# A two-layer attention kernel on one core: its written-out schedule replaced by another (order of the queues, engines, buffers, GpSimd's waits, TensorE's fillers)

## The chip, the cores and the metric

One core of one Trainium2 chip runs the whole kernel. The metric is the time of one execution on the device in microseconds, the median of several runs. The engines are named as in the profile: PE (TensorE's matmuls), PEld (its weight loads), DVE (VectorE), ACT (ScalarE), POOL (GpSimd), SP (SyncE, which only issues DMAs here).

## The reference

x has 2048 tokens of 512 numbers in bf16. Two layers follow each other, and each layer is an A block and a B block with a residual sum around each:

```python
x = x + _A_ref(_layernorm(x), A_wq, A_wk, A_wv, A_wo, A_beta)
x = x + _B_ref(_layernorm(x), B_wqkv, B_w_phi, B_wo)
```

and then the same two lines again. A has 32 heads of 16 numbers and 4 segments of 512 tokens. Within a segment it is causal softmax attention; beside it stands a memory (M, z) that the segments before have summed up, and a gate per head mixes the two:

```python
logits = einsum('bhqd,bhkd->bhqk', qs, ks) * scale + mask
a_dot  = softmax(logits) @ vs
a_mem  = (phi(qs) @ M) / (phi(qs) @ z + 1e-06)
o = g * a_mem + (1 - g) * a_dot
M = M + phi(ks).T @ vs;  z = z + sum(phi(ks))
```

with phi(t) = t + 1 where t > 0 and exp(t) elsewhere. B is linear attention over all tokens: queries and keys go through a 16x16 matrix per head, then softmax(t) and softmax(-t) side by side; kv and z are sums over all tokens, and o = (phi_q @ kv) / (phi_q @ z + 1e-06). Both blocks end in a product with a 512x512 matrix.

## The kernel before, in words

All of x lies in SBUF (`X`, 16 tiles of 128 tokens). The program is written as a list of 3416 small operations, numbered in the order in which the Python code adds them; an operation is one instruction of DVE, ACT, POOL or a DMA, or a few matmuls. In each layer the code goes through four segments: LayerNorm (`ln`: statistics, rstd by POOL's pow, xn on DVE, then a transpose by DMA or by PE), Q, K and V (`a_proj`), score products, Exp and masks and the product with V (`a_att`), the memory (`a_state`, `a_mem`), the output product and the residual sum (`a_out`); then for B the keys (`b_keys`), queries (`b_queries`) and, when all tokens are summed, the output (`b_out`). The output of B of the first layer is spread over the second layer's segments.

What an engine does next is not decided by the order of the Python code. Four tables are written out in the file, and `replay` reads them:

- `ORDER` lists the numbers of all operations. Each engine's queue (PE, ACT, DVE, POOL, SP) is the operations on it in this order, and each queue runs strictly in order. A number with 10000 added is interleaved, two matmuls at a time, with the PE operation before it. A negative number is a filler: matmuls on the zero tile `warm` (line 1431), whose result nobody reads; -401 stands for 25 of them.
- `ENGINE` has a letter for each of the 568 operations that could run on more than one engine (a, d, p, s for ACT, DVE, POOL, SP).
- `SLOTS` has the number of the buffer, or the PSUM bank, for each tile in the order of use. An operation waits until all users of the buffer's tile before are done.
- `AFTER` has pairs (x, y): operation x waits for y as well. In all pairs x is on POOL and y on DVE.

`finalize` makes semaphores of all this. The lines that the times below are told by:

```python
k, p = int(next(slots), 36), t.pool
...
self.queues[op.on].append(op.i)
...
for x, y in AFTER:
    ops[x].need.add(y)
```

Operations that the prediction speaks of, by number: 0, 1, 4, 5 load the first four tiles of x (X0 and X2 by ACT's queue, X1 and X3 by SP's, 128 KB each); 2 and 3 load the halves of `WA_k` (256 KB, ACT and SP), 6 and 7 those of `WA_q`, 8 and 9 those of `WA_v`; 10 loads beta (8 KB, ACT). SP alone loads 11 (X4 to X7, 512 KB), 12 (`wphi`, 16 KB), 13 and 14 (the raw B weights, 512 KB each), 15 (`WA_o`), 16 (`WB_v`), 17 and 18 (X8 to X11, X12 to X15) and 19 (`WB_o`). 20 sets `warm` to zero, 81 and 82 clear the two `ktok` buffers (line 767), all on DVE. 84 is the first K product, which reads both halves of `WA_k`. In `a_att`, the mask of the odd keys (line 1110) is one of those that may run on DVE or POOL; the mask of the even ones (line 1113) is always POOL's. Line 520 is the helper that issues every matmul, 579 the copy out of PSUM, 585 the DMA transposes, 601 PE's transposes, 1104 the Exp of the scores.

## Time and profile before

| | |
|---|---|
| time, median of 3 runs | 479.87 us (479.76 to 480.22) |
| span of the profiled execution | 479.8 us, which stands for its own time: 0.07 us under the median |
| busy: PE, DVE, ACT, POOL | 464.4, 428.1, 430.7, 261.0 us |
| weight loads (PEld) | 320.1 us |
| DMA | 35.86 MB, of which 6.32 MB read from HBM and 2.10 MB written |
| most instructions of one kind | L1104 Exp, 288 x 1068 ns, 282.4 us busy |
| masks of the odd keys, L1110 | 127 on POOL (697 ns each), 129 on DVE (364 ns each) |
| DMA transposes, L585 | 100, issue to landing 3.0 to 5.6 us, median 3.3 |

The page has one execution: busy time per engine, the span in 40 slices, DMA queues, the chain of work that ended last (followed back from the last instruction, at each step to what released it), the costliest groups of instructions by line, and the DMA issues. A group's row ends in its busy time, the mean length of one, and the engine's idle time ahead of it with what ended it. Consecutive instructions of an engine overlap a little, so busy time over count is less than the mean length. The end of a matmul is modelled, so PE's busy time holds some waiting too.

### The profile page before, as it was taken

Reading aid. Unit: us, or ns where it says so; the run is one execution under the profiler, and the core shown is the slowest. Engines: PE = TensorE matmul, PEld = TensorE weight load, DVE = VectorE, ACT = ScalarE, POOL = GpSimd, SP = SyncE. Lnnn points to the kernel's source line nnn. Section 1 sums busy time; section 2 is a strip of 40 time slices with the busy share of each in tenths; the row PEclk is TensorE's granted clock in tenths of the full one; section 3 lists DMA queues with packets and bytes.
Section 4 is the critical chain, followed back from the end, with each engine's and each line's share of the span. In section 5 each row is a group of like instructions: output and inputs, shape, how many; then the busy total and the mean of one; then the engine's idle time right before and its main releaser. Section 6 shows DMA issues by size and latency. Waiting matters only on the chain.

```text
span 479.8 us, 19249 instructions
## 1 busy us (share of the span) xinstructions
PE 464.4 (97%) x8324; PEld 320.1 (67%) x8324; DVE 428.1 (89%) x1021; ACT 430.7 (90%) x668; POOL 261.0 (54%) x420
## 2 busy tenths in 40 slices
PE   8999989999999999999999999999999999999997
PEld 7776667667856567557687666766865657665763
DVE  6999999989998988599999899999998879978785
ACT  3999999999999999986799899899999999999743
POOL 3577657646756576410246485784776578761100
PEclk9999999999999999999999999999999999999999
DMA  8978752225411232232257407236145112402376
GB/s 264 160 196 132 127 78 46 46 48 78 59 23 25 46 68 47 19 39 47 55 88 93 62 9 124 58 53 81 39 56 89 25 25 48 76 19 55 69 128 187
DMA packets 115091, 35.86 MB, mean 75 GB/s; under 512 B 106816, under 2 KB 115008, under 8 KB 115008
## 3 DMA queue, kind: packets, MB, share of 16 engines
q1 hardware_dynamic: 113184, 33.06, 39.9%
q10 hardware_dynamic: 1824, 1.58, 1.0%
q8 instruction: 65, 1.06, 0.9%
q14 instruction: 18, 0.15, 0.1%
HBM read 6.32 MB, written 2.10 MB: 18 GB/s over the span
## 4 chain that ended last, share of the span: by engine, by line
PE 40%; DVE 25%; ACT 22%; DMA 8%; POOL 3%; issue 1%; POOLq 0%; DVEq 0%
PE PS L520 38%; ACT PT L1104 16%; DVE stats L801 4%; DMA OT<-O 3%; ACT Ek L1200 3%; DVE xn L817 2%; DVE X L1165 2%; DMA EQ<-xn 2%; POOL PT L1113 2%; DVE Vt L1228 1%; DVE D L1110 1%; DMA xA<-xn 1%; DMA xB<-xn 1%; PE PS L1431 1%; DVE O L1139 1%
## 5 line engine op out<-in xcount | busy, mean ns | idle before, releaser
L1104 ACT ACTIVATE PT<-PS 128x1024 bf16<-128x1024 f32 x288 | 282.4, 1068 | 6.5 <-PE PS L520 5.6
L1110 POOL TENSOR_TENSOR D<-PT,modd 128x256 bf16<-128x256 bf16 x127 | 87.2, 697 | 41.7 <-ACT PT L1104 29.5
L1113 POOL TENSOR_SCALAR_AFFINE_SELECT PT<-PT 128x512 bf16<-128x512 bf16 x128 | 83.2, 658 | 48.1 <-DVE D L1110 43.3
L520 PEld LDWEIGHTS PS<-VT,PT 128*128 128x128 bf16 x2048 | 74.7, 96 | 18.7 <-POOL PT L1113 3.8
L520 PE MATMUL PS<-VT,PT 128*128 128x17 bf16 x2048 | 81.7, 171 | 1.5 <-POOL PT L1113 0.6
L520 PE MATMUL PS<-QT,K 32*128 32x64 bf16 (+2 forms) x2176 | 74.8, 213 | 1.1 <-ACT PT L1104 0.6
L520 PE MATMUL PS<-VT,D 128*128 128x17 bf16 x512 | 59.8, 170 | 0.0
L520 PEld LDWEIGHTS PS<-QT,K 32*128 32x128 bf16 x2176 | 40.4, 93 | 20.3 <-ACT PT L1104 10.0
L1110 DVE TENSOR_TENSOR D<-PT,modd 128x256 bf16<-128x256 bf16 x129 | 45.1, 364 | 2.1 <-ACT PT L1104 2.0
L520 PEld LDWEIGHTS PS<-VT,D 128*128 128x128 bf16 x512 | 43.2, 96 | 0.0
L1228 DVE TENSOR_TENSOR Vt<-PS,Zk 128x1024 bf16<-128x1024 f32 (+1 forms) x34 | 38.9, 1159 | 1.1 <-ACT Zk L1216 0.6
L801 DVE BATCH_NORM_STATS2 stats<-X 128x6 f32<-128x512 bf16 x56 | 37.6, 683 | 1.1 <-DMA X<-in_A_x_dram 0.7
L1200 ACT ACTIVATE Ek<-PS 128x512 bf16<-128x512 f32 x64 | 36.8, 648 | 1.6 <-PE PS L520 1.4
L1207 POOL TENSOR_TENSOR Vt<-Ek 128x512 f32<-128x512 bf16 x24 | 28.2, 1175 | 17.4 <-ACT Ek L1200 15.1
L520 PE MATMUL PS<-WA_k,xA 128*128 128x256 bf16 x256 | 36.6, 273 | 0.8 <-DVE xA L907 0.5
L1165 DVE TENSOR_TENSOR X<-X,PS 128x512 bf16<-128x512 bf16 x50 | 33.5, 678 | 4.3 <-PE PS L520 4.0
L1304 POOL COPY O<-rho 128x512 bf16<-128x512 bf16 x26 | 16.2, 642 | 38.7 <-DVE rho L1297 35.4
L520 PE MATMUL PS<-xA,WA_q 128*128 128x128 bf16 x512 | 36.4, 219 | 0.7 <-DMA xA<-xn 0.5
L520 PE MATMUL PS<-WA_v,xA 128*128 128x256 bf16 x256 | 36.3, 273 | 0.3 <-DMA xA<-xn 0.3
L520 PE MATMUL PS<-WA_o,OT 128*128 128x512 bf16 x128 | 32.1, 380 | 1.3 <-DMA OT<-O 0.7
L520 PEld LDWEIGHTS PS<-xA,WA_q 128*128 128x128 bf16 x512 | 30.0, 98 | 4.8 <-issue 1.0
L817 DVE TENSOR_SCALAR xn<-X,mv,rstd 128x512 bf16<-128x512 bf16 x64 | 28.6, 466 | 4.1 <-POOL rstd L813 1.7
(158 smaller groups left out, 983.5 us busy)
## 6 DMA issues: line engine op xcount, KB each, us to landing
X<-in_A_x_dram SPq DMA_DIRECT2D x3, 512.0 KB, 11.7
out_dram<-X SPq DMA_DIRECT2D x12, 128.0 KB, 1.8
EQ<-in_B_wqkv_dram SPq DMA_DIRECT2D x2, 512.0 KB, 4.9
OT<-O SPq DMA_TRANSPOSE x42, 3.2
WB_v<-in_B_wqkv_dram SPq DMA_DIRECT2D x1, 512.0 KB, 10.9
WA_o<-in_A_wo_dram SPq DMA_DIRECT2D x1, 512.0 KB, 4.1
WB_o<-in_B_wo_dram SPq DMA_DIRECT2D x1, 512.0 KB, 4.9
out_dram<-X ACTq DMA_DIRECT2D x4, 128.0 KB, 2.3
```

The lines of the kernel that those rows point to most:

```text
L520: return e.matmul(o, l, r, start=st, stop=sp, tile_position=(basep(l), basep(o)))
L801: self.dve(lambda e, t=t, src=src: e.bn_stats(self.stats[:, t, :], src()), 0.603, [held() if held else R("X", t)], [R("stats", t)], name=" ...
L817: self.dve(lambda e, t=t, n=n, xn=xn: e.tensor_scalar(xn.ap[:, n], self.X[:, t, :], self.mv[:, t, 0:1], self.rstd[:, t:t + 1], op0=ALU.sub ...
L1104: self.act(lambda e, st=st, pt=pt: e.activation(pt.ap[:].rearrange("p b c -> p (b c)"), self.ps[:, st.slot[0] * 512:st.slot[0] * 512 + 102 ...
L1110: self.either(lambda e, d=d, k=k, pt=pt: e.tensor_tensor(d.ap[:, :, k, :].rearrange("p b (z c) -> p b z c", z=2), self.ends(pt.ap[:, :, 25 ...
L1113: self.pool(lambda e, q=quarters: e.affine_select(q(), q(), [[0, 4], [1, 128]], ALU.is_ge, 0.0, base=0, channel_multiplier=-1), 0.6, [pt() ...
L1139: self.dve(lambda e, r1=r1, view=view, nt=nt, g=g, o=o[ts]: e.tensor_tensor(o.ap[:, 0:nt, g, :].rearrange("p i (h d) -> p i h d", d=DH), v ...
L1165: self.dve(lambda e: e.tensor_tensor(X[:, t, :], X[:, t, :], self.bank(gen), ALU.add), 0.6, [R("X", t), gen()], [R("X", t)], name="resid")
L1200: self.act(lambda e, sgn=sgn, Ek=Ek, gen=gen: e.activation(Ek.ap[:, sgn, :], self.bank(gen), ACT.Exp, scale=1.0 - 2.0 * sgn), 512, [gen()] ...
L1207: self.pool(lambda e, Ek=Ek, sums=sums: e.tensor_tensor(sums(), *(Ek.ap[:].rearrange("p s (h j) -> p s h j", h=H)[:, :, :, 8 * k:8 * k + 8 ...
L1228: self.dve(lambda e, w=w, n=n, Vt=Vt, Zk=Zk, gen2=gen2: e.tensor_tensor(self.signed(Vt)[:, w, :, 0:16], self.bank(gen2).rearrange("p (h d) ...
L1304: P.add(("act", "pool"), {"act": lambda e, dst=dst, src=src: e.activation(dst(), src(), ACT.Copy), "pool": lambda e, dst=dst, src=src: e.t ...
```

## The change

Only the four tables are replaced; no operation is added, removed or changed in shape, apart from the fillers.

| | before | after |
|---|---|---|
| fillers on PE (matmuls / groups) | 144 / 37 | 22 / 3 |
| pairs in AFTER | 119 | 224 |
| odd masks (L1110) DVE / POOL | 129 / 127 | 157 / 99 |
| K copies ACT / DVE | 16 / 12 | 12 / 16 |
| Q copies ACT / DVE | 22 / 10 | 19 / 13 |
| V copies ACT / DVE | 19 / 13 | 19 / 13 |
| kp copies ACT / DVE / POOL | 5 / 13 / 14 | 1 / 20 / 11 |
| lo copies ACT / DVE / POOL | 4 / 16 / 12 | 8 / 15 / 9 |
| bk.z ACT / DVE / POOL | 8 / 8 / 16 | 11 / 8 / 13 |
| bq.wide ACT / POOL | 6 / 26 | 7 / 25 |
| stores SP / ACT | 12 / 4 | 8 / 8 |
| operations on ACT, DVE, POOL, SP | 677, 1021, 416, 126 | 682, 1058, 378, 122 |

Half of the operations move by six places or fewer in ORDER. The order of the loads changes:

| queue | before | after |
|---|---|---|
| ACT | 0, 2, 4, 6, 8, 10 | 10, 0, 2, 6, 4, 8 |
| SP | 1, 3, 5, 7, 9, 11, 16, 18, 17, 12, two transposes of xn and one of ktok, 13, 14, ... | 1, 11, 7, 18, 5, 3, 17, 9, 12, 15, 13, a transpose of 13's tile, 19, 14, 16, a transpose of ktok, ... |

On DVE the first operations were 20, 33, 81, 82, 53 (the first statistics); they become 81, 34, 82, 35, 20, 53. The fillers left are 20 matmuls at the start and one each in two places later.

The diff, cut to the first lines of each table:

```diff
 ORDER = (
-    0, 20, 26, 1, 23, 21, 22, 2, 3, 24, 25, 28, 4, 5, 33, 81, 27, 6, 7, 82, 8, 9, 10, 11, 53, 16, 54, 18, 55, 60, 56, 17, 57, 12, 61, -401, 62, 63,
-    29, 58, 64, 65, 59, 67, 83, 84, 66, 74, 85, 89, 34, 86, 68, 103, 69, 70, 104, 87, 30, 90, 88, 105, 115, 91, 92, 116, 75, 31, 106, 93, 96, 102,
...
+    10, 1, 81, 21, 0, 2, 24, 6, 4, 8, 25, 11, 26, 34, 82, 7, 35, 22, 20, -323, 18, 5, 3, 53, 17, 9, 54, 55, 60, 12, 56, 33, 15, 27, 61, 62, 57, 63,
+    13, 58, 64, 59, 67, 65, 84, 66, 68, 69, 85, 70, 102, 103, 86, 83, 71, 104, 74, 89, 87, 105, 90, 75, 76, 72, 88, 37, 92, 115, 426, 40, 106, 91,
...
 AFTER = (
-    (102, 75), (184, 112), (389, 179), (186, 49), (181, 51), (195, 200), (196, 191), (213, 211), (1143, 208), (242, 747), (238, 388), (241, 745),
...
+    (22, 82), (27, 55), (28, 106), (29, 106), (31, 94), (32, 48), (56, 55), (63, 61), (70, 69), (77, 93), (83, 64), (165, 136), (180, 1131),
...
 ENGINE = (
-    "daddaaddpaapdaadaapapadpaaaapddpddppppddddddpppppdppdddppdppdapddaapadpdpdapapaadadddddapppaapppddpdpdddppddppdddddpdddppdddppddpdddddddapad"
...
+    "aaaapaadpaaaadapaadddaaddddadddddpddppdpppdddddpdpppdddpddddaadadaadadddpdadddaddadddddaaaaapappdddpppppddddddddddpdpddppddpddpddpddpdddadad"
...
 SLOTS = (
-    "00001102034050000001111220001314011020150131146020370011005829010415210021103310020610120211122330241300028009230110110312105101307121222110"
...
+    "03001300111421053331017003302140804215311222023010160120121100250113020210010900520143011012041131050810120001091120700251420206333114002206"
...
```

More of the change, by code (lines that the diff above doesn't have):

```diff
@@ L192 @@
+    "asasdsda"
 )
 SLOTS = (
[L194 to L197 removed]
@@ new lines @@
+    "71012030120130132014391002733105033312042001328010124501052601100139071220003220810230310102413132500030921215142601012023201050812202071203"
+    "23190313101011620011040012301105020018120420293676040100025011712132233205101200404152101033136137500145000311212037006712070102301013123030"
+    "02110543000640314003072021105002260110031700167805232112702230930005130000212061013115020222001181101013320907102103031123204381222206310322"
+    "03111234073351210123813010501140333603315120101232100040011562401022112011112010130050115332413030312100728160101425210040100092501004002532"
@@ L207 @@
+    "1326012716022160210172063012671062013"
 )
```

26 lines of the change are left out of this document (10 added, 16 removed), and 300 rows, old and new, of tables (AFTER, ORDER).

## The prediction

> **What bounds the kernel now.** I read the page first, for its span, its engine sums and the chain.
>
> ```profile
> span 479.8 us, 19249 instructions
> PE 464.4 (97%) x8324; PEld 320.1 (67%) x8324; DVE 428.1 (89%) x1021; ACT 430.7 (90%) x668; POOL 261.0 (54%) x420
> PE 40%; DVE 25%; ACT 22%; DMA 8%; POOL 3%; issue 1%; POOLq 0%; DVEq 0%
> ```
>
> Three engines are nearly full and the chain changes hands among them, so no one of them is "the" bound over the whole span. Hence the second view: busy time by stretch, cut at the first and the last score Exp (L1104) of each layer.
>
> ```profile
> 0.00:12.80 12.80, 11.13 (x118) 9.06 (x118) 9.09 (x28) 5.14 (x9) 4.70 (x20) 1.00 0.85 272
> 12.80:203.40 190.60, 184.88 (x3676) 128.15 (x3674) 175.10 (x434) 185.94 (x257) 121.09 (x190) 1.00 0.43 74
> 203.40:238.80 35.40, 35.02 (x403) 23.44 (x400) 32.84 (x66) 26.27 (x70) 5.04 (x8) 1.00 0.31 50
> 238.80:433.30 194.50, 190.31 (x3722) 132.24 (x3720) 177.55 (x434) 186.62 (x257) 126.86 (x196) 1.00 0.39 60
> 433.30:479.80 46.50, 43.02 (x424) 27.17 (x421) 33.55 (x61) 26.68 (x80) 3.27 (x6) 1.00 0.48 107
> ```
>
> Columns: stretch, its length, busy us of PE, PEld, DVE, ACT, POOL, then clock, DMA share, GB/s. In the first attention stretch ACT idles 190.6 - 185.9 = 4.7 us, in the second 194.5 - 186.6 = 7.9 us: whatever the order, those stretches can't get shorter by more than that unless ACT gets less work. Between the layers PE is full (35.02 of 35.40). Before 12.8 us ACT does little: the start is a delay that all three engines share.
>
> The third view is the timeline of the start (PE, PE, ACT; start us, us, what), with the piece of the chain that lies there; the fourth the DMA issues of the loads (KB each, us from issue to landing), with busy time and GB/s of the first microseconds.
>
> ```profile
> 1.04 5.18 PE L1431 MATMUL PS<-warm 128*128 128x240 bf16 x25 [1.04 <-DVE warm L702]
> 7.61 1.07 PE L520 MATMUL PS<-xA,WA_k 128*128 128x128 bf16 x16
> 12.82 1.96 ACT L1104 ACTIVATE PT<-PS 128x1024 bf16<-128x1024 f32 x2
> 7.67 4.88 PE PS L520 x80
> WA_k<-in_A_wk_dram SPq DMA_DIRECT2D x1, 256.0 KB, 3.7
> WA_v<-in_A_wv_dram SPq DMA_DIRECT2D x1, 256.0 KB, 7.1
> wphi<-in_B_w_phi_dram SPq DMA_DIRECT2D x1, 16.0 KB, 10.5
> 2.00:4.00 2.00, 2.00 (x12) 1.47 (x10) 1.16 (x3) 0.15 (x1) 0.00 (x0) 1.00 0.90 251
> 4.00:6.00 2.00, 2.00 (x12) 1.42 (x10) 1.81 (x7) 1.14 (x1) 0.56 (x1) 1.00 1.07 360
> 6.00:8.00 2.00, 1.37 (x17) 0.99 (x16) 1.33 (x4) 0.41 (x2) 0.82 (x2) 1.00 1.08 368
> ```
>
> wphi, 16 KB, takes 10.5 us to land: SP's loads land in turn, behind all bytes issued ahead. The loads run at 360 to 368 GB/s once they run. The K product at 7.61 is the head of a piece of the chain (7.67, 4.88 us), and the first Exp follows it at 12.82.
>
> **The change part by part.** Instructions and shapes stay; what moves are queues, engines, buffers, waits and fillers.
>
> *The start.* The first K product (operation 84) reads both halves of WA_k. SP issues the second half (operation 3) second now; afterwards sixth, behind X1, X4-7, half of WA_q, X12-15 and X3: with itself 128 + 512 + 256 + 512 + 128 + 256 = 1792 KB. ACT's 1032 KB of loads run beside it; the two queues' loads of equal size land together now, so I let them share: 2824 KB, 2.89 MB. By 4.0 us 0.53 MB have moved (251 GB/s for 2 us and a little before); the other 2.36 MB at 365 GB/s take 6.5 us: 10.5 us. A landing lags behind its bytes: half of WA_k by 0.2 us now, half of WA_v by 1.4 (issued at 2.7, landed 7.1 us later at 9.8; its 2.1 MB were through by 8.4). With 0.7 it is 11.2. Against 7.61 that is +3.6 us, on the path, since ACT's first Exp waits for this product's K and nothing else fills ACT. Bounds: were ACT's loads out of the way, 1.84 MB would be there by 7.6 us; then only ACT's new first load (beta, ahead of X0) and the longer DVE queue ahead of the first xn count, some +0.8. Above, +6. I take 3.6.
>
> *Fillers (L1431).* 144 matmuls become 22: 20 at the start, two later. Their busy time by stretch:
>
> ```profile
> 0.00:12.80 12.80, 5.26 (x26) 3.61 (x26) 1.00 0.85 272
> 12.80:203.40 190.60, 7.68 (x47) 4.04 (x46) 1.00 0.43 74
> 203.40:238.80 35.40, 2.17 (x18) 1.76 (x18) 1.00 0.31 50
> 238.80:433.30 194.50, 4.21 (x25) 2.00 (x25) 1.00 0.39 60
> 433.30:479.80 46.50, 3.95 (x29) 2.63 (x29) 1.00 0.48 107
> 209.41 1.39 PE L1431 MATMUL PS<-warm 128*128 128x240 bf16 x12
> 210.32 0.40 DVE L817 TENSOR_SCALAR xn<-X,mv,rstd 128x512 bf16<-128x512 bf16 x1
> 360.19 0.47 PE L1431 MATMUL PS<-warm 128*128 128x240 bf16 x3
> 362.11 0.27 PE L1431 MATMUL PS<-warm 128*128 128x240 bf16 x1
> ```
>
> Behind 12.8 us they are 18.0 us of busy time, most of it over waits: the twelve at 209.41 end at 210.8, and what follows transposes the xn that DVE ends at 210.72. Those at 360.19 and 362.11 stand before operations whose inputs were ready. Group by group, from the end of the latest input to the start of PE's next operation, I find 3.0 us, in 19 of 37 groups, in which a filler was in the way: 0.8 in the first stretch, 1.3 in the second, 0.8 at the end, 0.1 at the start. The fillers hide nothing else but the gap; with that cover gone PE simply waits.
>
> *Engines.* The masks (L1110) go from 127 on POOL and 129 on DVE to 99 and 157.
>
> ```profile
> L1110 POOL TENSOR_TENSOR D<-PT,modd 128x256 bf16<-128x256 bf16 x127 | 87.2, 697 | 41.7 <-ACT PT L1104 29.5 <-PE PS L520 4.9 <-DVE PhiQ L961 2.4
> L1110 DVE TENSOR_TENSOR D<-PT,modd 128x256 bf16<-128x256 bf16 x129 | 45.1, 364 | 2.1 <-ACT PT L1104 2.0
> L579 DVE CAST QT<-PS 128x512 bf16<-128x512 f32 x10 | 6.8, 683 | 1.2 <-PE PS L520 1.1
> ```
>
> DVE +28 x 45.1/129 = +9.8 us, POOL -28 x 87.2/127 = -19.2. K and Q copies, net seven from ACT to DVE at 6.8/10: +4.8 DVE; all other moves net to -0.4. DVE +14.2, ACT -0.9, POOL -24.7. By stretch (everything ORDER puts between those Exps, each at its group's mean) DVE gets +7.4, -2.6, +9.2 and +0.2 us; ACT -0.2, +1.9, -1.4, +0.2. So ACT's floor under the attention stretches stays within 1.4 us.
>
> *GpSimd's waits (AFTER).* 119 become 224, each a POOL instruction waiting for a DVE one.
>
> ```profile
> L1110 DVE TENSOR_TENSOR D<-PT,modd x129: 222/284/1245, 17.9 to 428.9; 128x256 bf16<-128x256 bf16 x129
> L817 DVE TENSOR_SCALAR xn<-X,mv,rstd x64: 317/408/1252, 5.4 to 439.6; 128x512 bf16<-128x512 bf16 x64
> L817 DVE TENSOR_SCALAR xn<-X,mv,rstd 128x512 bf16<-128x512 bf16 x64 | 28.6, 466 | 4.1 <-POOL rstd L813 1.7 <-ACT rstd L808 1.6 <-DMA xA<-xn 0.3
> ```
>
> Some DVE instructions run up to 1.25 us where their median is 0.28: the mean exceeds the median by 80 ns on 129 masks (10.3 us) and by 58 on 64 xn (3.7 us); over all such lines I count some 20. More waits should take away some two thirds, -14: about what the moves add. I set the net at 0, between +14 (nothing saved) and -6 (all saved). Behind a waiting POOL instruction stand masks and the rstd of the next LayerNorm; POOL's 54% with 24.7 us less work hides that.
>
> *Transposes and TensorE's fetches.* Seven DMA transposes stand in the chain, each near 5 us (first and last):
>
> ```profile
> 16.79 5.36 DMA xA<-xn
> 376.42 4.86 DMA xB<-xn
> PEld PS L520 <- issue: 15.3, 61, 0.6
> ```
>
> ORDER leaves fewer operations between a layer's transposes and their first users than now (medians 38 to 32.5 for xn, 33 to 29.5 for O), so I grant no gain: 0, between -4 and +4. [...] I take 0. SLOTS and the stores (SP 12, ACT 4 to 8 and 8) cost 0 to 0.5.
>
> **Sum.** Start +3.6. First stretch: ACT -0.2, fillers -0.8: -1.0 (bounds -4.7, +4). Between layers: PE's queued work without fillers falls 33.7 to 32.8, -0.9, DVE's -2.6 lets -0.3 more through: -1.2 (-3, 0). Second stretch: ACT -1.4, fillers -1.3, -0.5 for shorter POOL chains: -3.2 (-9, +5). End: fillers -0.8, last store on ACT +0.3: -0.5. Together -2.3: 479.8 - 2.3 = **477.5 us**. The execution's span of 479.8 is 0.07 under the runs' median of 479.87; I don't correct for it.
>
> **Rivals.** *A, no loss at the start* (the two queues don't share, or DVE and ACT find other work): the sum loses +3.6 and gives 473.9. For it: DVE has X4-7 earlier; against: wphi's 10.5 us. *B, the start's loss eats all that the rest gains* (rest -3.6): 479.9, within 0.2%, which is what a measurement here can tell from no change. *C, slower: PE starts slow.*
>
> ```profile
> 1.84 0.48 DVE L767 MEMSET ktok<- 128x512 uint32 x1
> ```
>
> The first 25 fillers take 5.18/25 = 207 ns each, the twelve at 209.41 only 116: PE runs at half speed until about 6 us. Afterwards fillers start later (the memset of warm, which they read, stands behind both 0.48 us memsets of ktok), and PE idles from about 8.4 to 11.2 for WA_k. If it is slow there, the piece of 4.88 us grows by 207/116 - 1 = 0.8 of itself: 477.5 + 3.9 = 481.4; the result is slower than before once this costs over 3.3 us (2.3 that the sum gains, and 1.0). [...] *D, slower: the added DVE work isn't paid for by the waits*: +14.2 on an engine that holds 25% of the chain, +3.5: 481.0.
>
> **Chances.** Forecast 0.35, A 0.14: faster 0.49. B 0.17. C 0.20 and D 0.14: slower 0.34. The likeliest case alone runs from 475 to 478.9. The range for all reaches from A with a third of the second stretch's bound (471) to C and D nearly together (484).
>
> **What would show it.** The first WA_k product (x16 on PE) at 10.5 to 12 us, ACT's first Exp at 16 to 17; at 7.6 and 12.8 A holds, and a filler-like 107 ns between the first K matmuls shows C. L1431 x22, and stretch lengths of about 189.6, 34.2, 191.3 and 46. L1110 on DVE with a mean under 320 ns: waits work; at 364 D. The prediction fails above all if the second attention stretch gets longer, or if the first shrinks by more than ACT's 4.7 us.

## The result: 1.1% slower

| | before | after |
|---|---|---|
| time, median of 4 runs each | 480.05 us (479.76 to 480.42) | 486.24 us (483.82 to 486.83) |
| ratio after / before | | 1.011, 95% interval 1.0082 to 1.0139 |
| span of the profiled execution | 479.8 us | 485.1 us |
| granted clock in it | 1.000 | 0.972 (0.972 to 0.982 in the four runs) |

The prediction was 477.5 us, faster. The time lies outside its range (471 to 484), on the other side of the kernel before. Here and below, medians, clocks and ratios leave out four executions that were far slower than the others of their kernel (one each of the 98 wide fillers, the thin fillers, the changed kernel with the first loads as before, and the splice). The page of the kernel after, its first rows:

```profile
span 485.1 us, 18991 instructions
PE 459.6 (95%) x8202; PEld 315.7 (65%) x8202; DVE 423.7 (87%) x1058; ACT 431.5 (89%) x669; POOL 237.4 (49%) x382
PEclk8888998999999998999999999999999998999999
PE 54%; ACT 23%; DVE 14%; DMA 6%; issue 1%; SPq 1%; POOL 0%; DVEq 0%
```

Every engine but ACT has less busy time than before, and the span is 5.3 us longer. TensorE's share of the chain has grown from 40% to 54%, and in the third row, which gives the granted clock in tenths, it is no longer 9 everywhere; in the kernel before it was 1.00 in all five stretches. The same cut into stretches (length, busy us of PE, PEld, DVE, ACT, POOL, clock, DMA share, GB/s; line 1104 is now 1112):

```profile
0.00:19.29 19.29, 11.69 (x112) 9.72 (x112) 9.44 (x30) 7.29 (x14) 5.68 (x20) 0.82 0.83 251
19.29:214.67 195.38, 187.22 (x3633) 129.63 (x3633) 172.19 (x450) 186.10 (x256) 110.68 (x171) 0.96 0.36 65
214.67:248.38 33.71, 32.16 (x381) 21.47 (x380) 30.48 (x63) 27.19 (x73) 4.60 (x9) 1.00 0.25 49
248.38:439.50 191.12, 188.48 (x3693) 130.66 (x3693) 177.55 (x457) 184.44 (x251) 113.17 (x177) 0.99 0.37 61
439.50:485.10 45.60, 40.01 (x393) 24.19 (x389) 34.01 (x62) 26.50 (x81) 3.29 (x6) 1.00 0.48 110
```

| stretch | before | forecast | after | after - before, forecast | after - before, measured |
|---|---|---|---|---|---|
| start | 12.8 | 16.4 | 19.3 | +3.6 | +6.5 |
| first attention | 190.6 | 189.6 | 195.4 | -1.0 | +4.8 |
| between layers | 35.4 | 34.2 | 33.7 | -1.2 | -1.7 |
| second attention | 194.5 | 191.3 | 191.1 | -3.2 | -3.4 |
| end | 46.5 | 46.0 | 45.6 | -0.5 | -0.9 |

Three of the five terms came out within 0.5 us of the forecast. All of the error, 8.7 us, lies in the first two, and these have the lowest clocks, 0.82 and 0.96.

**The start.** The timeline of TensorE and ScalarE (start us, us), then the DMA issue of the second half of WA_k:

```profile
2.29 3.81 PE L1439 MATMUL PS<-warm 128*128 128x240 bf16 x20 [2.29 <-DVE warm L710]
12.22 3.57 PE L528 MATMUL PS<-xA,WA_k 128*128 128x128 bf16 x32 [2.77 <-DMA WA_k<-in_A_wk_dram]
19.29 1.02 ACT L1112 ACTIVATE PT<-PS 128x1024 bf16<-128x1024 f32 x1
```

```profile
WA_k<-in_A_wk_dram SPq DMA_DIRECT2D x1, 256.0 KB, 8.5
```

Issued at 3.63, landed at 12.1: 0.9 us later than the 11.2 of the sum. Some 0.6 us of that (an estimate from the bytes moved in each two microseconds) is that the bytes ahead of it came later, above all at the start:

```profile
2.00:4.00 2.00, 1.71 (x9) 1.32 (x10) 0.24 (x3) 0.00 (x0) 0.10 (x1) 1.00 0.63 140
```

140 GB/s, where the same two microseconds had 251 before. The rest is that it landed 1.0 us after its bytes, not 0.7. The 32 matmuls take 3.57/32 = 112 ns each, the mark that the prediction gave for a slow TensorE.

**The first attention stretch.** Two pieces of the chain of work, and TensorE's waits between 20 and 36 us:

```profile
21.82 5.96 DMA K<-ktok
28.13 4.85 DMA xA<-xn
```

```profile
PE PS L528 <- DMA xA<-xn: 2.0, 1, 2.0
PE PS L528 <- DMA K<-ktok: 0.7, 1, 0.7
```

Comparing the n-th score Exp of both traces, the delay grows from 6.5 us at the first to 10.2 at the nineteenth (50.5 us), stays between 9.2 and 13.0 from there on and is 11.4 at the last. So the first 31 us of it lose nearly 4 us, and there TensorE waits for transposes done by DMA. Before, the transpose of K (operation 125) was issued at 18.2 and landed at 23.1 us, that of the first xn (352) at 16.8 and 22.2. Now they land at 27.8 and 33.0. Most of this lateness they inherit: K's copy is ready 4.6 us later than before (at 21.8), and xn 9.8 us later (at 26.6), of which the late start is 6.5. From ready to landed they take 6.0 and 6.4 us, where it was 5.9 and 5.4. SyncE's own timeline shows what stands ahead of them:

```profile
17.59 2.10 SPq L593 DMA_TRANSPOSE OT<-EQ  x1
19.74 0.57 SPq L595 DMA_DIRECT2D WB_o<-in_B_wo_dram  x1
20.36 0.50 SPq L595 DMA_DIRECT2D EQ<-in_B_wqkv_dram  x1
20.90 0.51 SPq L595 DMA_DIRECT2D WB_v<-in_B_wqkv_dram  x1
21.82 1.91 SPq L593 DMA_TRANSPOSE K<-ktok  x1
23.77 4.32 SPq L593 DMA_TRANSPOSE OT<-EQ  x2
28.13 4.21 SPq L593 DMA_TRANSPOSE xA<-xn  x2
```

Three loads of 512 KB (WB_o among them, whose first user comes at 235.7 us), and three transposes of raw B weights, which hold the queue until their load has landed (the first until 17.57 us). With the late start the queue adds little to the delay; what it costs when the start is on time is measured below.

**The clock.** In this trace it falls to half five times, three times for 6.83 us and twice for 3.41. In windows of 3.41 us from 5.59 on, these are the ones around the first two losses and the third (columns as above):

```profile
5.59:9.00 3.41, 1.01 (x11) 0.55 (x10) 2.69 (x9) 0.53 (x1) 1.46 (x3) 1.00 1.08 363
9.00:12.41 3.41, 0.64 (x7) 0.40 (x7) 1.54 (x5) 1.08 (x3) 0.88 (x2) 0.50 1.11 349
12.41:15.83 3.42, 3.42 (x34) 3.35 (x33) 1.35 (x4) 1.16 (x2) 0.00 (x0) 0.50 1.13 322
29.48:32.89 3.41, 1.61 (x42) 1.08 (x39) 1.82 (x5) 3.01 (x4) 1.87 (x4) 1.00 1.10 177
32.89:36.31 3.42, 3.19 (x48) 2.22 (x49) 2.98 (x9) 0.65 (x2) 1.27 (x3) 0.50 0.65 122
36.31:39.72 3.41, 3.41 (x36) 2.76 (x36) 1.63 (x6) 2.37 (x4) 2.90 (x5) 0.50 0.00 0
67.03:70.44 3.41, 2.95 (x78) 2.25 (x75) 3.41 (x8) 2.73 (x4) 1.61 (x3) 1.00 0.57 114
70.44:73.85 3.41, 3.41 (x46) 1.99 (x42) 3.01 (x9) 2.93 (x5) 0.64 (x1) 0.50 0.29 52
456.15:459.56 3.41, 2.46 (x36) 2.12 (x36) 2.37 (x6) 2.41 (x11) 0.61 (x1) 1.00 0.31 60
```

The first two falls follow a window in which TensorE did little: 1.01 us of work before 9.00, 1.61 before 32.89. But 2.95 us of work before 70.44 also brought a half clock, and only 2.46 from 456.15 on did not. The busy time does not separate these windows; how much of the array the matmuls used does (a busy TensorE in these rows can hold some waiting, since the ends of matmuls are modelled). I count the columns that each matmul streams, times the share of the array's rows and columns that it uses (a score matmul of 64 columns on 32 of 128 rows counts 16; all matmuls here use all 128 columns of the array, so only the share of its rows varies; some 8000 fit in a window, by a filler's 240 columns every 102 ns):

| window of the kernel after | columns in use | clock of the next window |
|---|---|---|
| 5.59 | 1488 | half |
| 179.67 | 2592 | half |
| 67.03 | 2693 | half |
| 404.95 | 2762 | half |
| 29.48 | 2816 | half |
| 363.99 (the lowest other one) | 3288 | full |

In the kernel before no window from 10 us to 475 us has under 3472. Over the eight traces of this case that lack no matmul record, between 10 and 475 us, 23 windows at full clock were followed by a half clock, all with at most 3172 columns, and more than 1000 were not, all with at least 2974. Of the half windows in these traces, all that the full clock followed had at least 3120 (of about 4000 possible, by the 200 ns from one filler to the next before 5 us), and some with up to 3224 were followed by another half one. Of the eight half windows of the kernel after, two follow the gap at the start and two the wait for xn; the other four (from 70.44, 183.08 and 408.36) follow windows in which TensorE was busy for at least 2.9 of 3.41 us.

### The profile page after: what moved, and what is told of

Same layout as the page of the kernel before. It is cut to its first block, busy times and chain, and to the rows that moved or that the text cites. A ratio compares the mean times of both kernels' runs of the same rounds, so it can differ in the third digit from the quotient of the medians.

```text
span 485.1 us, 18991 instructions
## 1 busy us (share of the span) xinstructions
PE 459.6 (95%) x8202; PEld 315.7 (65%) x8202; DVE 423.7 (87%) x1058; ACT 431.5 (89%) x669; POOL 237.4 (49%) x382
## 4 chain that ended last, share of the span: by engine, by line
PE 54%; ACT 23%; DVE 14%; DMA 6%; issue 1%; SPq 1%; POOL 0%; DVEq 0%
PE PS L528 53%; ACT PT L1112 16%; DVE Vt L1236 2%; ACT Ek L1208 2%; DMA WA_k<-in_A_wk_dram 2%; DMA K<-ktok 1%; DMA OT<-O 1%; DMA xA<-xn 1%; DMA EQ<-xn 1%; DVE O L1350 1%; DVE X L1173 1%; DVE stats L809 1%; DVE KV L1265 1%; ACT K L1293 1%; PE PS L609 1%
## 5 line engine op out<-in xcount | busy, mean ns | idle before, releaser
L1121 POOL TENSOR_SCALAR_AFFINE_SELECT PT<-PT 128x512 bf16<-128x512 bf16 x128 | 82.1, 651 | 65.4 <-DVE D L1118 45.4
L1118 POOL TENSOR_TENSOR D<-PT,modd 128x256 bf16<-128x256 bf16 x99 | 67.7, 691 | 34.4 <-ACT PT L1112 15.7
L528 PE MATMUL PS<-QT,K 32*128 32x64 bf16 (+2 forms) x2176 | 75.9, 215 | 1.9 <-ACT PT L1112 0.6
L1118 DVE TENSOR_TENSOR D<-PT,modd 128x256 bf16<-128x256 bf16 x157 | 47.6, 318 | 4.6 <-ACT PT L1112 2.5
L1236 DVE TENSOR_TENSOR Vt<-PS,Zk 128x1024 bf16<-128x1024 f32 (+1 forms) x34 | 39.1, 1158 | 1.1 <-PE PS L528 0.4
L1215 POOL TENSOR_TENSOR Vt<-Ek 128x512 f32<-128x512 bf16 x24 | 28.3, 1181 | 22.6 <-ACT Ek L1208 13.4
L528 PE MATMUL PS<-WA_o,OT 128*128 128x512 bf16 x128 | 32.2, 380 | 0.3 <-DVE OT L587 0.2
L528 PE MATMUL PS<-WB_o,OT 128*128 128x512 bf16 x128 | 31.7, 379 | 0.3 <-DMA OT<-O 0.3
```

The lines of the kernel that those rows point to most:

```text
L528: return e.matmul(o, l, r, start=st, stop=sp, tile_position=(basep(l), basep(o)))
L1118: self.either(lambda e, d=d, k=k, pt=pt: e.tensor_tensor(d.ap[:, :, k, :].rearrange("p b (z c) -> p b z c", z=2), self.ends(pt.ap[:, :, 25 ...
L1121: self.pool(lambda e, q=quarters: e.affine_select(q(), q(), [[0, 4], [1, 128]], ALU.is_ge, 0.0, base=0, channel_multiplier=-1), 0.6, [pt() ...
L1215: self.pool(lambda e, Ek=Ek, sums=sums: e.tensor_tensor(sums(), *(Ek.ap[:].rearrange("p s (h j) -> p s h j", h=H)[:, :, :, 8 * k:8 * k + 8 ...
L1236: self.dve(lambda e, w=w, n=n, Vt=Vt, Zk=Zk, gen2=gen2: e.tensor_tensor(self.signed(Vt)[:, w, :, 0:16], self.bank(gen2).rearrange("p (h d) ...
```

## The experiments

Theories: W, the clock falls for want of fillers and costs time (W-area: judged by columns in use; W-busy: by instructions in flight); L and A, the late loads with and without an effect; S, transposes wait in SyncE's queue; G, fillers only stand in the way; F, removing fillers shifts TensorE's instruction fetches, which was a guess (the page of the kernel before has a DMA queue of instructions, 65 packets with 1.06 MB; that TensorE waits for them no run shows). All ratios are to the kernel before, run on the same chip beside them.

| kernel | median us | ratio, 95% interval | granted clock, median |
|---|---|---|---|
| after + 98 wide fillers | 487.28 | 1.0137 (1.0113 to 1.0162) | 0.996 |
| after + 294 thin fillers | 495.15 | 1.0317 (1.0290 to 1.0343) | 0.970 |
| before - 119 fillers | 486.81 | 1.0137 (1.0116 to 1.0159) | 0.975 |
| before, 119 fillers thin | 482.54 | 1.0064 (1.0042 to 1.0086) | 0.989 |
| before, 119 fillers doubled | 486.96 | 1.0140 (1.0120 to 1.0159) | 1.000 |
| before, first loads as after | 486.57 | 1.0139 (1.0119 to 1.0159) | 0.991 |
| before, 512-KB loads ahead of transposes | 494.16 | 1.0282 (1.0261 to 1.0304) | 0.979 |
| after, first loads as before | 483.12 | 1.0073 (1.0045 to 1.0100) | 0.986 |
| after, SyncE mended (first try) | 491.48 | 1.0229 (1.0206 to 1.0252) | 0.979 |
| after, both | 485.96 | 1.0105 (1.0085 to 1.0124) | 0.980 |
| after, both + 32 fillers | 489.24 | 1.0181 (1.0155 to 1.0208) | 0.988 |
| after, loads + SyncE (second try) | 481.63 | 1.0038 (1.0018 to 1.0058) | 0.982 |
| the same + 23 fillers | 482.91 | 1.0062 (1.0039 to 1.0085) | 0.993 |
| the same + the 119 of before | 490.95 | 1.0216 (1.0195 to 1.0237) | 0.990 |
| after + the 119 of before | 492.11 | 1.0235 (1.0200 to 1.0270) | 0.988 |
| spliced: first layer before, second after; two sets | 484.36, 484.15 | 1.0086 (1.0057 to 1.0115), 1.0088 (1.0065 to 1.0111) | 0.989, 0.991 |
| after without GpSimd's waits | 494.05 | 1.0288 (1.0264 to 1.0311) | 0.976 |

Lines shift between kernels by the length of their tables; tiles tell the groups apart. Each kernel has one profile, of one execution; of the thin fillers added to the changed kernel none is read.

### Fillers added to the changed kernel

```diff
 ORDER = (
-    ... 58, ... 65, ... 84, ... 137, ... 404, ...
+    ... -257, 58, ... -65, 65, ... -385, 84, ... -72, 137, ... -296, 404, ...
```

and seven groups more. In the thin variant each added filler becomes three matmuls of 16 columns.

> The changed kernel with 98 more fillers of 240 columns, put where its trace shows TensorE waiting or hardly using the array (44 of them between 6 and 12 us, 4 at 27.8, 18 at 31 to 33, 5 at 68, 14 at 176 to 181, 10 at 364 to 366, 3 at 406). Theory W (windows): the granted clock halves for one 3.41-us window after each window in which too little of the array was used, and this is what made the start 2 us and the first attention stretch some 5.5 us longer than forecast. Then the clock is 1.00 throughout, the first K product stays at 12.2 us, the first score Exp comes at 17.4 instead of 19.3, the first attention stretch falls from 195.4 to about 190, and the span from 485.1 to 477.7 (476 to 479.5), ratio to before 0.996. Theory L (late loads): the 6 us come from the late loads and from what follows them; the clock falls while TensorE has nothing to do and costs nothing. Then the clock rises but the time stays at 484 to 486. Theory G (in the way): fillers only delay; 98 x 0.10 us less what lies in waits gives 487 or more.

> The same as the kernel with 98 more fillers, but each of these added fillers is three matmuls of 16 columns in place of one of 240: about the same time on TensorE (three weight loads of some 30 ns each against 100 ns), a fifth of the columns streamed through the array. It tells what a window is judged by. If by TensorE having instructions in flight (theory W-busy), the clock stays at 1.00 and the time is that of the kernel with 98 wide fillers, near 477.7. If by the array cells in use (theory W-area: columns times the share of rows and columns of the array; in the changed kernel's trace all windows up to 2816 such columns were followed by a half clock, none from 3288 on), the clock falls in the same places as in the changed kernel, and the time is 484 to 487. Theory L: 484 to 486 as well, but then the wide fillers give the same.

W was right about the clock (0.996) and about the first Exp (17.59 us for 17.4), and wrong about the time: 487.3 us is what theory G had expected. TensorE's timeline shows where the start's gain went:

```profile
30.20 1.03 PE L529 MATMUL PS<-WA_k,xA 128*128 128x256 bf16 x4 [4.08 <-DMA K<-ktok]
```

TensorE came earlier to the same late transpose and waited 4.1 us for it instead of 0.7 (the loads ahead of it landed 1.4 us later, too, in this execution). The 1.7 us gained at the start were lost there; what the other fillers cost and brought was not measured apart. With thin fillers the clock fell to 0.966 to 0.983 where the wide ones had held it at 0.995 to 1.00: W-area, not W-busy. But there are three times as many of them, so the time proves nothing.

### Fillers taken from the kernel before

```diff
-    29, 58, 64, ... 158, -22, 209, ... 335, -33, 166, ...
+    29, 58, 64, ... 158, 209, ... 335, 166, ...
```

for all groups but -401; and, in another kernel, the same fillers kept but thinner:

```diff
-    ... self.ps[:, b * 512 + 272:b * 512 + 512], self.warm[:], self.warm[:, None, 0:120].to_broadcast([128, 2, 120])
+    w = 120 if n == 25 else 8
+    ... self.ps[:, b * 512 + 272:b * 512 + 272 + 2 * w], self.warm[:], self.warm[:, None, 0:w].to_broadcast([128, 2, w])
```

> The kernel before, without its 119 fillers behind the start (the first 25 stay). Theory W-area: counted over its trace without these fillers, stretches of 3.41 us with under 3280 columns appear around 164.5 to 171, 207.1 to 208, 355.4 to 359 and 398 to 400.4; the first and the third are longer than a window and must cost at least one half window each, so the clock is 0.98 to 0.99 and two to four half windows of up to 1.7 us each stand against the 3.0 us by which the fillers were in the way: 478 to 482, about 480. The prediction's view (fillers hide nothing but the gap, with that cover gone TensorE simply waits): 479.8 - 3.0 = 476.8, clock 1.00.

> The kernel before with all its 144 fillers in place, but the 119 behind the first 25 stream 16 columns in place of 240. Instructions, their number and order are untouched, so TensorE's instruction fetches lie where they lay; the fillers take some 30 ns in place of 100. Theory W-area: the columns in use fall as if the fillers were gone, the clock halves in 5 to 8 windows (0.975 to 0.982), and the time is 483.5 to 487, as without fillers (486.8). Theory F (removing fillers shifted the fetches, and that cost the 6.6 us, as added fillers cost time by shifting them): 477 to 480.5, whatever the clock does. Theory W-busy (instructions in flight keep the clock up): clock 1.00, 478 to 480.

Removing them costs 6.6 us, where the prediction had a gain of 3.0. W-area's own sum (478 to 482) missed as well: six windows ran at half clock in the profiled execution, for the two to four expected. Windows of that kernel:

```profile
166.08:169.50 3.42, 1.98 (x89) 1.70 (x87) 3.23 (x11) 3.42 (x6) 1.63 (x3) 1.00 0.02 5
169.50:172.91 3.41, 2.59 (x86) 2.11 (x83) 2.68 (x9) 3.13 (x6) 2.47 (x5) 0.50 0.43 82
```

The clock falls near three of the four places where the count over the old trace had put it (half from 169.5, 360.6 and 405.0 us; counted 164.5 to 171, 355 to 359 and 398 to 400; not at 207). The thin kernel has the same instructions in the same places and some 8 us less of TensorE's time (119 x 70 ns), yet is 2.3 us slower, with half clocks in the same places: that goes with the lower clock (0.989 for 1.000), with number and order of the instructions as they were. It is less than W-area's 483.5 to 487 and more than F's 480.5 at most. The other 4.3 us of the removal go with more windows that fall (clock 0.975 against 0.989); at one clock the two kernels take one time, 485.5 us at 0.978 here and 485.7 at 0.979 without fillers, which leaves little for F. Why fewer windows fall with thin fillers than with none is open. Its eight runs differ by how many windows fall: six with a clock of 0.986 to 0.989 took 481.3 to 483.3 us, two with 0.978 and 0.982 took 485.4 and 485.5. Over 113 runs of the changed kernel and of all experiments, each against the mean of its own set, 0.51 us of time go with each us of clock lost (correlation 0.72). That is a correlation: a late transfer costs time and empties a window too. The times of a kernel with half windows spread more here: twelve runs of one below, at clocks of 0.978 to 0.989, from 480.0 to 484.8 us, nineteen of the kernel before from 478.7 to 481.1.

### What a filler costs

Each of the 36 groups twice as long:

```diff
-    ... -22, 209, ... -197, ...
+    ... -38, 209, ... -389, ...
```

> The kernel before with each of its 36 filler groups behind the start twice as long (238 matmuls in place of 119). The clock is 1.00 already, so only their cost is left: 119 x 0.10 = 11.9 us more TensorE work. If they lie in waits as the first 119 do (3.0 us of theirs were in the way by the prediction's count): 482 to 484. If the first ones had used up the waits, nearly all of it counts, up to the share that the chain gives TensorE: 486 to 490.

With the clock at 1.00 all the same, 119 more fillers cost 6.8 us, 57 ns each of their 102. The fillers of the kernel before sit in waits, and there is little room beside them. Then the same 119 in the other order, each group ahead of the operation that it preceded:

> The changed kernel with the 119 fillers of the kernel before put back, each group ahead of the same TensorE operation as there. Theory W-area: the half windows at 183 and 408 us go, those at the start, at 33 and at 70 stay; the granted clock rises from 0.977 to about 0.986, some 4 us less of clock lost. Within one kernel's runs I find 0.6 us of time per us of clock lost (78 runs of 13 kernels), so -2.5, against 3 to 5 us of fillers in the way in an order that was not made for them: 485.5 to 488.5. If the fillers' absence is the whole cause of the loss and they cost nothing: 480. If fillers only stand in the way: 490 or more.

The clock rose to 0.988, as W expected, and the time to 492.1: 5.9 us of loss, and above the 485.5 to 488.5 expected. The groups chosen for the gaps of the old order are mostly in the way in the new one.

### The first loads

In the changed kernel, the order of before at the same places (and the reverse in the kernel before):

```diff
-SP: 1, 11, 7, 18, 5, 3, 17, 9, 12    ACT: 10, 0, 2, 6, 4, 8
+SP: 1, 3, 5, 7, 9, 11, 18, 17, 12    ACT: 0, 2, 4, 6, 8, 10
```

> The kernel before with the order of the first loads of the changed kernel (SyncE: X1, X4-7, half of WA_q, X12-15, X3, half of WA_k, X8-11, half of WA_v, wphi; ScalarE: beta, X0, half of WA_k, X2, halves of WA_q and WA_v), all else as it was. By the prediction's step: the first K product at 11.2 to 12.2 us, the first Exp 4 to 6.5 us later, and nothing makes it up: 484 to 486.5. Rival A (the start's loss is hidden): 480 to 481. More than 487 would say that the late loads cost more than the late start.

> The changed kernel with the first loads in the order of the kernel before (SyncE: X1, half of WA_k, X3, halves of WA_q and WA_v, X4-7, X12-15, X8-11, wphi; ScalarE: X0, half of WA_k, X2, halves of WA_q and WA_v, beta). All else stays, the fillers too. Theory W with the late start: the first K product moves from 12.2 to about 8, TensorE has no long wait before it, the clock does not fall there, and the first Exp comes at about 13.3 in place of 19.3: -6 us, 479 (477 to 481); the half windows at 33 to 40 and 70 to 77 remain if their causes (a wait for transposed xn, a gap at 68) remain. Theory A (the late start is hidden by other work, so that nothing hangs on it): 484 to 486.

Put into the kernel before, the new order of loads costs 6.3 us, at the upper end of what was expected. The first Exp comes at 20.04, 7.2 us later where 4 to 6.5 were expected, and the stretch behind it makes up nothing; it stays at its 190.6 us (in this profile the second layer is the quicker one, its attention stretch 192.2 us for 194.5):

```profile
0.00:20.04 20.04, 13.37 (x118) 11.10 (x118) 9.47 (x28) 5.25 (x9) 4.68 (x20) 0.74 0.70 211
20.04:210.67 190.63, 181.97 (x3652) 128.27 (x3676) 174.82 (x433) 185.93 (x257) 120.85 (x190) 1.00 0.41 70
```

Taken out of the changed kernel it gives only 3.1 us back, less than W and more than A had expected, though the first Exp came at 13.4. TensorE's waits between 20 and 34 us:

```profile
PE PS L528 <- DMA K<-ktok: 6.7, 1, 6.7
```

The transpose of K, ready at 16.1, was issued at 21.0 behind the three loads and landed at 28.1. With the late start it had landed at 27.8: the late start and the queue delay the same transposes, and either alone makes the 19th Exp 7 to 8 us late (table below).

### SyncE's queue

The numbers of operations behind wphi, in the second and better try:

```diff
+        q, first = self.queues["sp"], [1, 3, 5, 7, 9, 11, 18, 17, 12, 125, 13, 352, 343, 14, 140, 15, 426, 357, 436, 427, 16, 19]
+        at = sorted(q.index(x) for x in first)
+        for k, x in zip(at, first):
+            q[k] = x
```

The first try had 125, 352, 343, 15, 13, 426, 140, 14, 427, 436, 16, 357, 19 there.

> The changed kernel with SyncE's queue alone in another order behind wphi (operation 12): the transposes of K (125), of two xn (352, 343) stand ahead of the 512-KB loads of the raw B weights, WA_o, WB_v and WB_o (13 to 16, 19) and of their transposes (426, 427, 436). Theory S (SyncE's queue): the first attention stretch is long because these transposes wait in it; in the changed kernel 125 lands at 27.8 us and 352 at 33.0, against 23.1 and 22.2 before, and TensorE waits for both (the first at 27.83, 0.7 us; the second at 33.12, 2.0 us). With the late start kept, 125 is issued when its copy is ready (21.8) and lands near 25, 352 is ready at 26.6 and lands near 30: -3 us, 483 (481 to 485), and the half clock at 33 to 40 goes or gets shorter. Theory W (clock alone, from the few fillers): no change, 485 to 487.

> Both: the first loads in the order of the kernel before, and the transposes ahead of the 512-KB loads. With the first loads alone the first Exp came at 13.4 us, but TensorE then waited 6.7 us (to 28.1) for the transpose of K, whose copy was ready at 16.1: it was issued at 21.0 behind three 512-KB loads. Theory S: this wait goes nearly whole, 483.6 - 5 = 478.5 (477 to 480.5), and the first attention stretch falls from 197.5 to 192.5. Theory W: the wait costs little by itself and the half clock stays elsewhere: 482 to 484.

> Both orders, and 32 fillers of 240 columns at the places where the changed kernel hardly used the array (5 at its 68 us, 14 at 176 to 181, 10 at 364 to 366, 3 at 406). With the first loads alone the granted clock was half at 180.1 to 183.5 and 361.0 to 371.3, 13.7 us in all. Theory W+S: clock 1.00, and of the up to 6.8 us of TensorE's work lost there some 3 come back: 475.5 (474 to 477.5), faster than both kernels. Theory G (fillers in the way): nothing is gained, 478 to 480 as without them.

> The kernel before with the four 512-KB loads 15, 13, 19 and 14 moved ahead of the first three transposes (352, 125, 343) on SyncE, all else as it was. Theory S: 2.1 MB at 365 GB/s are 5.7 us of loading ahead of the transposes, which now are issued at 16.8 to 20.8 and land at 22.2 to 23.9; they would land some 2 to 4 us later, and the first, 5.4 us of it in the chain of work, delays everything behind it: +3 us, 483 (481.5 to 485). Against S: transposes pass the loads or other work covers them: 480.

All four expectations missed, the first two for one reason: my order put the next two transposes of K (140, 357) and the first of O behind the weights. SyncE in the kernel with both edits:

```profile
31.14 1.23 SPq L597 DMA_TRANSPOSE OT<-EQ  x1
32.42 1.34 SPq L597 DMA_TRANSPOSE K<-ktok  x1
33.80 0.58 SPq L599 DMA_DIRECT2D EQ<-in_B_wqkv_dram  x1
34.42 5.11 SPq L597 DMA_TRANSPOSE OT<-EQ  x2
39.58 0.58 SPq L599 DMA_DIRECT2D WB_v<-in_B_wqkv_dram  x1
40.21 2.76 SPq L597 DMA_TRANSPOSE K<-ktok  x1
```

The transpose at 32.42 (140) was ready at 26.5; the other, 357, was ready at 32.2, was issued at 40.2 and landed at 46.3. Fillers on top (the third) raised the clock from 0.980 to 0.988 and the time by 3.3 us. The kernel before, with four such loads ahead of its first transposes, lost 14 us where I had expected 3: TensorE waits 3.0 us for xn and 6.4 us for a transposed weight, and the clock is at half for 20 us. The second try:

> The changed kernel with the first loads as before, and SyncE's queue behind wphi mended a second time. The two earlier edits of it made the transposes 125, 352 and 343 land at 21 to 28 us but pushed 140 and 357 back: ready at 26.5 and 32.2, they were issued at 32.4 and 43.0, behind 426, 427 and 436, which hold the whole queue until their 512-KB load has landed. Now the order is 125, load 13, 352, 343, load 14, 140, load 15, 426, 357, 436, 427, loads 16 and 19: no transpose stands behind a wait of over 2 us. Theory S (the first attention stretch is long for transposes that wait on SyncE): the 18th Exp comes 2 to 3 us later than before in place of 8.2 (loads alone) or 10.6 (the first mending), and the time is 478.5 (476.5 to 481). If the queue's order only moves the wait around and another thing (DVE's xn, the clock) holds these 30 us: 482 to 486.

> The changed kernel with the mended loads and SyncE queue and only 23 fillers, in four places: 7 at its 61 to 67 us, 8 at 171 to 178, 8 at 356 to 359, where a window of 3.41 us holds as few as 2045, 1738 and 1924 of the columns whose threshold lies between 2816 and 3288. W-area: two to three half windows fewer, 3.4 to 5 us less clock lost, -2 to -3 against at most 2.3 us of fillers in the way: 480 (479 to 481.5). Theory G: +1 to +2, 483.

> The same 119 fillers in the changed kernel with the mended loads and SyncE queue (481.6 us, clock 0.98 to 0.99). W-area: clock 0.993 to 1.00, 4 us less lost, -2.5, and 3 to 5 us in the way: 481 to 484. If the fillers are worth what they were worth in the kernel before (0.4% there, thin fillers against wide ones): 478.5 to 480.

481.63 us: 4.6 less than the changed kernel, 1.5 of it by the queue (the intervals of the two ratios overlap), but 0.6 above the range expected. The delay of the n-th score Exp against the kernel before, in us, tells where the time goes:

| kernel | first | 18th | 19th | last of the first stretch |
|---|---|---|---|---|
| before, first loads as after | 7.2 | 7.3 | 7.3 | 7.2 |
| after | 6.5 | 9.0 | 10.2 | 11.4 |
| after, first loads as before | 0.6 | 7.1 | 8.2 | 7.6 |
| after, loads + SyncE (second try) | 0.3 | -0.4 | 4.7 | 6.3 |

The expectation's 18th, counted from zero, is this 19th: 4.7 us for the 2 to 3 expected. The two last kernels differ in SyncE's queue alone, and up to the 18th Exp the mended queue wins back all that the other loses. Then one step loses 5.1 us. There TensorE stands still for 3.6 us, which the list of its waits puts under "issue" (63 matmul records are missing near 39 us, but its weight loads are complete, and there is none from 39.1 to 42.5 us):

```profile
PE PS L532 <- issue: 3.6, 1, 3.6
35.14 1.18 SPq L599 DMA_DIRECT2D WB_v<-in_B_wqkv_dram  x1
36.36 0.51 SPq L599 DMA_DIRECT2D WB_o<-in_B_wo_dram  x1
36.91 1.80 SPq L597 DMA_TRANSPOSE OT<-O  x1
```

The next weight load, at 42.48, is for the product of WA_o with the transposed output O. O was ready at 35.46; its transpose was issued at 36.91, behind the two 512-KB loads that the mended order had put last, and landed at 42.42 (5.5 us; 3.2 in the kernel before). So theory S holds for this wait too: the second mending moved one more transpose behind loads. Without it some 476.5 us would be left, an estimate (481.6 - 5.1) that no run tests. The two attention stretches of this kernel:

```profile
13.12:209.53 196.41, 182.12 (x3608) 127.47 (x3633) 171.79 (x451) 186.44 (x256) 111.27 (x172) 0.97 0.39 71
243.24:432.96 189.72, 184.18 (x3664) 129.97 (x3693) 177.52 (x457) 184.28 (x251) 113.18 (x177) 1.00 0.35 61
```

The clock of 0.97 in the first one is in part a consequence: the half window from 42.03 follows that wait. Adding 23 fillers brought the clock to 0.993 and no time (482.91, as G expected), adding 119 cost 9.3 us. No version that ran beats the kernel before.

### The second layer, and GpSimd's waits

The splice takes the first 1712 places of the old ORDER and the new order, engines, buffers and waits for all operations that are left. Without AFTER, the other kernel has `AFTER = ()`.

> The kernel before up to place 1712 of its ORDER (the end of the first layer: 1691 operations with their engines, buffers, waits and fillers), and from there the changed kernel's order, engines, buffers and waits for the other 1725 operations, without fillers. If the gains behind the first layer (second attention stretch 191.1 against 194.4 us, end 45.6 against 46.5) belong to the second layer's order by themselves: 480.1 - 4.2 = 476 (474.5 to 477.5), faster than both, and all of the loss sits in the first layer. If they were only time made up that the first layer had left waiting: 479 to 481.

> The spliced kernel once more (the kernel before up to the end of the first layer, then the changed kernel's second layer without fillers), for stretch lengths that its first profile could not give. If the second layer's order is worth what it showed in the changed kernel: between 35.4, second attention stretch 191, end 45.6, and the missing gain sits in half windows (each 0.7 to 1.1 us per us lost; 484.4 us at a clock of 0.989). If its gain there was time made up: second stretch 194 or more at the same clock.

> The changed kernel without its 224 pairs in AFTER: GpSimd waits for data alone. By the prediction's step the waits keep GpSimd off DVE's instructions and save some 14 us of DVE time: the mean of L1110's masks on DVE rises from 318 to 360 ns or more, 157 x 42 = 6.6 us on them alone, DVE's busy time by some 14 us, and the time by 2 to 5 us: 488 to 491. If the waits save nothing: 484 to 487, the mean within 10 ns of 318.

The splice from its second profile:

```profile
12.81:203.47 190.66, 185.00 (x3677) 128.09 (x3675) 175.48 (x434) 186.22 (x257) 121.01 (x190) 1.00 0.42 73
203.47:243.17 39.70, 35.84 (x407) 24.88 (x404) 32.58 (x65) 27.36 (x74) 4.67 (x9) 0.96 0.27 44
243.17:434.89 191.72, 187.65 (x3693) 129.81 (x3693) 177.33 (x456) 184.47 (x251) 113.77 (x176) 1.00 0.35 60
434.89:480.48 45.59, 40.01 (x393) 24.19 (x389) 33.99 (x62) 26.27 (x81) 3.30 (x6) 1.00 0.51 110
```

The second layer's gain is its own: 191.7 and 45.6 us behind an old first layer, 3.7 less than before together. The seam takes 4.3 back (39.70 against 35.4), so the 476 us expected did not come, and by its ratio the whole is 0.9% slower. This profile is of the fastest of its six runs (482.24 us, clock 0.996), and where the others lose 2 us more is not shown. Without GpSimd's waits:

```profile
PE 460.9 (93%) x8202; PEld 314.7 (64%) x8202; DVE 436.1 (88%) x1058; ACT 433.3 (88%) x669; POOL 239.4 (49%) x382
L1097 DVE TENSOR_TENSOR D<-PT,modd 128x256 bf16<-128x256 bf16 x157 | 52.6, 349 | 4.1 <-ACT PT L1091 2.5 <-PE PS L507 1.5
```

against, with them, 423.7 us on DVE and

```profile
L1118 DVE TENSOR_TENSOR D<-PT,modd 128x256 bf16<-128x256 bf16 x157 | 47.6, 318 | 4.6 <-ACT PT L1112 2.5 <-PE PS L528 2.1
```

The 224 waits together save 12.4 us of DVE's time, and 7.8 us of the kernel's, more than the 2 to 5 expected.

## Why the prediction failed, step by step

- **Start, +3.6: right mechanism, too small.** It measured +6.5, past its own bound of +6. WA_k landed 0.9 us later than worked out, some 0.6 of it because the sum took the rates of the old trace (251 GB/s at first, where 140 ran). The other 1.9 us are rival C, which the prediction kept at 0.20 and did not add: from the K product to the first Exp it took 7.1 us for 5.2, at half clock to 15.83. That is a little over half of the 3.42 us from 12.41 to 15.83, in which TensorE was busy throughout at a clock of 0.50. That the delay isn't hidden is shown by the kernel before with these loads, +6.3.
- **Transposes, 0: the step that failed in the first attention stretch.** I compared how many operations lie between a transpose and its user in ORDER. I did not follow SyncE's queue past the loads, though the table of the change listed it: the 512-KB loads 19, 14, 16 and the weights' transposes, with their waits, now stand ahead of 125, 352 and 343. With the first loads as before, this queue makes the 18th Exp 7.1 us late, and the mended one brings it 0.4 early. In the changed kernel the late start hides most of that, and the delay grows by 3.7 us up to the 19th Exp, for the 0 (-4 to +4) of the sum: the first xn lands 10.8 us later than before, of which the start is 6.5, a later xn on DVE 3.3 and the queue 1.0. How much of the 3.7 is the waits (2.7 us of TensorE's) and how much the half clock behind them (32.89 to 39.72) is not separated. The other 1.2 us of the stretch come later, where the clock falls at 70 and 183 us; and the gain of 1.0 that the sum had did not come. The 0 for the "issue" waits of TensorE's weight loads, which the prediction called fetches, rests on no run, and none shows what they are: 15.3 us in 61 waits before, 20.5 us in 65 after.
- **Fillers, "hide nothing else but the gap": wrong.** The gap is hidden, the clock isn't. Without its 119 fillers the kernel before is 6.6 us slower, and with thin ones in their places 2.3; my 3.0 us of gain had the wrong sign. Rival C had the mechanism, but at the start alone.
- **DVE and GpSimd's waits, net 0: right, on the safe side.** L1110's mean is 318 ns (under the 320 that I had named), and DVE ends 4.4 us below before, inside the bounds of +14 and -6. Rival D is out. The 14 us forecast for going from 119 waits to 224 was not measured by itself; the 12.4 us are what all 224 save.
- **Between, second stretch, end: right in size,** to 0.5 us each, and the second layer's gain stands by itself in the splice. But it is in part luck: the sums for the second stretch and the end count 1.3 and 0.8 us for the fillers that go, and in the kernel before without fillers these two got 0.6 and 0.25 us longer. Something else gained as much; what it was no run shows.
- **ACT's floor: right, and of no use.** I bounded the first stretch from below by ACT's work; its upper bound of +4 rests on no row, and +4.8 was measured.
- **The profiled execution's own time.** The results list a time 1.7 to 2.0 us above the span for every run, so the span of 479.8 belongs to an execution of about 481.5, not to one at the median. The forecast is hardly touched (the median less 2.3 is 477.6), but the profiles differ by 5.3 us where the medians differ by 6.2.

The parts can't be added up. The late loads and the late queue overlap, so that mending the loads alone gives back only 3.1 us, and both also empty the windows that then fall to half. How much of the changed kernel's clock loss (0.023 of 486 us, 11 us, some 6 us of time by the slope of 0.51) comes from the missing fillers, and how much from those waits, stays open, beyond the count of four half windows each in one execution; no filler set that I tried was worth its price there.

## What to carry to other kernels

Where a queue is served in order, follow every moved load past each transfer behind it, and name which of those its engine waits for; a count of operations in a schedule does not show it. When two delays overlap, mending one gives little back and looks like a wrong theory: compare the n-th instruction of a kind in both traces, and look at each step where the delay jumps. Before taking fillers out, count the array use of each 3.41-us stretch of TensorE without them, and compare it with the least that any window of the same kernel has with them (3472 of some 8000 columns in the kernel before, at a clock of 1.00): here the clock fell near three of the four places that such a count named, and the time rose by 6.6 us. The same 119 fillers cost the changed kernel 5.9 us: they paid in the gaps that they were chosen for.

## What the hardware showed that I had not expected

- In these traces the granted clock goes with the array's cells in use, not with TensorE's busy time: in the kernel after, a window 86% busy (from 67.03, 2.95 of 3.41 us, 2693 columns) was followed by a half clock, one 72% busy (from 456.15, 2.46 us, 4864 columns) was not. Of the windows at full clock in eight traces (10 to 475 us), none with over 3172 of some 8000 columns was followed by a half clock, and every one with under 2974 was; in between both were seen.
- One kernel (the second SyncE try) runs from 480.0 to 484.8 us with clocks from 0.989 to 0.978; the kernel before, with no window under 3472 columns in its trace, has 1.00 in nearly all runs.
- A filler cost 57 ns of its 102 where the clock was 1.00 without it (119 more in the kernel before, 6.8 us).
- A DMA transpose issued behind three 512-KB loads took 7.1 us to land (21.0 to 28.1, the changed kernel with the first loads as before) against 3.1 without them (17.9 to 21.1, the one with both edits).
